# Attention and a gated product on one core: batch 3 as one block of 448 tokens, and a new order on every engine

## The chip, the cores and the metric

The kernel runs on one core of a Trainium2 chip. The metric is the device time of that core in microseconds, taken as the median of several executions. TensorE (PE) does the matrix products, VectorE (DVE), ScalarE (ACT) and GpSimd (POOL) the work on single elements, and SyncE (SP) issues the loads, the stores and the transposes by DMA.

## The reference

Inputs are q, k and v of shape 4 x 12 x 448 x 64 (batch, head, position, width), `w_in` (768 x 2048) and `w_out` (2048 x 768), all float32.

```python
scores = q @ k.T / sqrt(64)            # per batch and head; later positions are masked
attn = softmax(scores)                 # over the keys
x = (attn @ v) laid out as [4*448, 12*64]       # 1792 tokens x 768
h = x @ w_in                           # 1792 x 2048
g = h * (1 / (1 + exp(-1.702 * h)))
out = g @ w_out                        # 1792 x 768
```

## The kernel before

**Precision.** Each large product is done in 16 bits with both factors split into a high and a low part, as three products (high x high, high x low, low x high) that add up in PSUM. The splits are scaled by powers of two taken from sums of squares of the inputs. Weights and inputs are converted and split on DVE and ACT on the way in.

**Tokens and blocks.** The 1792 tokens are 28 chunks of 64, seven in a batch. `TUNE["groups"]` cuts them into nine blocks in this order: 0 = batch 0, chunks 0-3 (256 tokens); 1 = batch 1, chunks 0-2 (192); 2 and 3 = batch 2 (256 and 192); 4 and 5 = batch 3 (256 and 192); 6 = batch 1, chunks 3 and 4 (128); 7 = batch 1, chunks 5 and 6 (128); 8 = batch 0, chunks 4-6 (192). Blocks 0 and 1 do their attention in 32 bits with transposes on PE; the later blocks use 16-bit splits and transposes by DMA.

**Work of a block.** First come six units of attention (`unit`, one per pair of heads): scores on PE (`ps_s`), maxima on DVE (line 1122), exponentials on ACT (line 1136), splitting into `p`, its transpose `PT`, the product with v (`ps_v`, line 1302), and the result as `xT`. Then `moe(n)`: eight times `h_slice`, each for 256 columns of `w_in`, and then `out_tile` for each 128 tokens. One `h_slice` runs two halves `t` of 128 columns, and each half is 18 pairs of matmuls (`halves`, line 410: two matmuls side by side, each on 64 columns of weights) whose width is the number of tokens of the block. Both halves lie in one bank of `ps_h`, so a block of w tokens has 2w columns there, which are then read by four operations: tanh on ACT (line 1401), a multiply on DVE (line 1406), the high part of `gT` on ACT or DVE (468, 470) and its low part on DVE (473). One `out_tile` (line 1442) has two halves `nh` of 384 output columns; each takes 48 pairs of matmuls 384 wide in eight groups of six pairs, and group f needs pair f of the 16 pieces of `w_out`, which `w_out_split` splits on DVE into `wob` (line 473, 128x768).

**Buffers.** `xT` and `gT` are rings of seven chunks; a block sits at `first_at[n] % 7`. `ps_h` has three banks, `ps_o` and `ps_s` two, `PT` two buffers.

**What sets the order.** Each piece of work is an operation with a number. The table `ORDER` lists all of them, each with its engine (S, P, A, D, G for SP, PE, ACT, DVE, POOL); each engine runs its own in that order, and waits at an operation until its inputs are there. All loads go through SP's queue in table order.

Of the kernel before, what the change touches and what calls it, by code (L numbers as in the profile page):

```python
# [49 lines left out]
    wi2=2.63,  # L50
    parts=(((0, 1), (1, 3), (3, 6)), ((0, 3), (3, 6))),
# [3 lines left out]
1D 3G 2A 60S 0G 4S 45S 57S 9S 541G 14S 108S 61P 49S 5A 62A 6D 7A 84P 27S 8D 47S 58P 85A 59A 111S 10D 82P 491S 11A  # L55
46S 70P 12A 83D 13D 15A 159S 63P 71D 162S 73D 16A 109P 64D 447S 66D 74A 17D 93P 444S 72A 110D 65A 18D 86P 67A 75P
77D 96D 19P 28A 78D 94D 32S 87D 133P 89D 97A 20D 29D 79P 48S 95A 76D 21P 68P 88A 112P 22D 90A 30D 80A 98P 24D 100D
23D 113A 31D 134A 432S 121P 69A 101D 25A 99D 135P 122D 114P 124D 50S 91P 136D 123A 160P 115D 117D 125A 144P 26D 118A
436S 116A 137P 161A 163P 92A 102P 145D 164A 215S 147D 184P 146A 140D 210S 128D 148A 186P 138D 494S 129D 185D 141A
119P 103D 434S 172P 33A 187D 165P 139A 34D 81P 538S 173D 35A 168D 126P 166D 433S 175D 188P 169A 151D 120D 195P 167A  # L60
36D 174A 437S 51P 176A 191D 189D 152D 127A 196D 104P 198D 192A 52D 37P 190A 179D 228S 105D 197A 573S 53P 130P 216D
199A 545S 448P 54D 38D 217A 180D 202D 445P 56D 55D 131D 39P 149P 617D 40D 449D 106A 153P 218D 446A 42D 469P 107D
211A 142P 203D 450P 219D 150A 233S 467P 143A 435S 132P 212D 154A 470A 451D 155P 43A 213D 453D 170P 214D 177P 468A
457P 156D 452A 181P 251S 171A 41D 44D 178A 471P 193P 157A 200P 182A 454A 495P 458D 229A 204P 158D 246S 478P 194A
# [12 lines left out]
606A 342S 659D 603A 348S 536A 321D 607P 356A 665P 609D 296D 537D 777S 322D 660A 592P 361A 666P 661D 375S 608A 357D
362A 323P 610D 672P 671D 314D 358D 667A 611P 363D 394A 399S 673P 668D 612A 442D 680D 364D 613P 669A 674P 343A 670D
405S 329P 986D 344A 614D 675P 371D 372D 615A 349D 681P 778S 345A 616D 335P 350D 676A 682P 346D 351A 341P 677D 376A
381S 683P 352D 678A 347P 377D 684P 387S 679D 378A 400D 353P 987P 685A 379D 359P 988P 686D 395A 365P 406D 779S 989P  # L80
687D 396A 1003P 366D 688D 367P 990P 397D 995P 382A 368D 411S 370D 369D 1004P 373D 991A 374D 383D 689A 996P 992D 384D
1005P 993A 690D 780S 388A 997P 385D 1006P 691A 389D 998P 401A 407D 380P 390D 723P 999A 408D 402A 391D 386P 412A 994D
392P 403D 781A 1011P 413A 409D 398P 559S 1012P 1000D 561S 414A 404P 692D 1013P 562S 1001A 415D 410P 1007A 560S 1014P
693A 782D 1002D 417S 724P 784G 1008D 542S 783G 694D 1019P 1009A 786A 543S 1010D 416P 1015A 1020P 428D 721D 788G 787D
695A 725P 1016D 429G 859S 563A 1051D 789G 696D 1021P 856S 1017A 1348D 564P 1027P 697A 857S 1018D 565D 1022P 567D
566G 858S 698D 568A 726P 815S 785G 418D 1023A 1035P 569D 699A 1028P 790S 546A 419D 1036P 547A 700D 420A 727P 1024D
764S 549A 701D 1029P 765S 548A 421D 728P 1025A 570S 860A 702D 422P 1037P 554D 861D 1026D 703A 863G 423D 555P 729P
862D 766S 556D 558D 557G 865A 704D 424P 1043P 763S 775A 867G 425D 866D 1030P 854A 427D 426D 730P 1281D 922S 868G
776D 571A 921S 1044P 430D 855D 802P 924S 705A 791P 1038P 923S 805D 731A 1045P 706D 767A 869S 743P 803D 806A 794D
707A 792D 768P 827P 572D 732S 744P 804A 795A 816P 769D 807G 708D 1046P 793A 1191S 771G 925A 796G 745P 431D 808D  # L90
1031A 1346D 770G 709D 894S 772A 926D 733P 797D 1032D 928G 710D 864G 811A 746P 1193S 798A 927G 800A 773D 809A 734P
711A 1194S 812D 1039A 747P 799D 774S 712D 1033A 735P 1195A 801D 817D 713A 810D 748P 819D 845S 830D 930A 828D 736P
818A 714D 844S 932G 820A 829A 749P 842S 931D 821G 831A 843S 722D 715A 1034D 737P 933G 822D 1040D 1073S 1196A 832G
1052D 750P 716D 823A 1192S 825A 1200A 833D 824D 738P 826D 836A 1076S 1349D 1347D 1361D 751A 834D 837D 717A 881P 813S
835D 1053P 1362D 1041D 1199A 718D 846A 870P 1054P 1075S 882D 1202A 884D 739P 838S 719A 873D 871D 1042D 883A 906P
720D 885A 895P 847P 1055P 1074S 874A 848D 886G 872A 850D 849D 740P 959S 1201A 851D 929G 1198A 875G 887D 1056P 852D
1197A 741A 934S 814P 888A 876D 1203D 890D 1047A 753P 877D 889D 879A 891D 853S 1077A 1057P 907D 909D 908A 878D 754P
880D 910A 896D 1078D 898D 897A 911G 1058P 742S 1048D 899A 1080G 1079D 892S 1049A 1081D 900G 912D 755P 915A 913D
1050D 1082A 1204P 839P 901D 916D 904A 1209S 1084G 756P 914D 902A 1083D 840A 1208S 905D 1059P 1085G 903D 841D 1211S
757P 1205D 917S 1207D 1206G 946P 935P 1929D 758P 1994D 947D 938D 1086S 948A 936D 1060P 949D 939A 2540D 937A 950A  # L100
# [191 lines left out]
def kernel(  # L292
# [1275 lines left out]
```

## Time and profile before

| | |
|---|---|
| time, median of 3 runs | 582.13 us (581.78 to 582.66) |
| the profiled execution's own time | 581.97 us |
| its span | 580.3 us |
| granted TensorE clock | 1.000 |

The span runs from the first to the last instruction of the profiled execution; its own time lies 1.7 us above. An engine's busy time is the time in which at least one of its instructions ran. Matmuls overlap, so what one costs in a stream is read from the starts of successive groups.

### The profile page before, as it was taken

The page shows a single profiled execution, that of the slowest core. Times are in us where ns is not written, and L with a number is a line of the kernel's source. Part 1 is how long each engine was busy: PE and PEld are TensorE (multiplying, and loading weights), DVE is VectorE, ACT ScalarE, POOL GpSimd, SP SyncE. Part 2 cuts the span into 40 slices and gives each one's busy share as a digit, 9 for nine tenths or more (in the row PEclk, how much of TensorE's full clock was granted, in tenths as well). Part 3 has the DMA queues.
Part 4 walks back from the last instruction along what each step waited for, and adds up shares of the span by engine and source line. Part 5 has one row for each costly group of instructions (what it writes and reads, how often), then busy time and mean ns, then how long its engine had stood idle before and what let it go on. Part 6 is the DMA issues. An engine that isn't in the chain of part 4 may idle for free.

```text
span 580.3 us, 24080 instructions
## 1 busy us (share of the span) xinstructions
PE 564.2 (97%) x10376; PEld 475.5 (82%) x10376; DVE 424.6 (73%) x1201; ACT 365.2 (63%) x879; POOL 60.8 (10%) x165
## 2 busy tenths in 40 slices
PE   6999979999999999999999999999999999999997
PEld 4778868988788998779977899778987978889965
DVE  3899999999998688778758759555887987823110
ACT  5899999899976566458746556364665555512210
POOL 2000000013120102101100103011102020000000
PEclk9999999999999999999999999999999999999999
DMA  8999659588997968899846967877758957620010
GB/s 267 268 275 371 199 165 334 180 190 161 187 194 152 155 124 155 141 164 170 155 71 130 154 122 111 130 157 132 119 110 141 139 97 113 107 61 3 16 28 28
DMA packets 228187, 86.70 MB, mean 149 GB/s; under 512 B 208880, under 2 KB 217840, under 8 KB 228080
## 3 DMA queue, kind: packets, MB, share of 16 engines
q1 hardware_dynamic: 228080, 85.16, 72.4%
q8 instruction: 81, 1.33, 1.0%
q14 instruction: 26, 0.21, 0.1%
HBM read 44.63 MB, written 5.51 MB: 86 GB/s over the span
## 4 chain that ended last, share of the span: by engine, by line
PE 78%; DVE 12%; DMA 4%; ACT 2%; issue 1%; SPq 1%; DVEq 0%; ACTq 0%
PE ps_o L1442 33%; PE ps_h L410 30%; PE ps_v L1302 5%; PE ps_s L1099 5%; DVE wob L592 2%; DVE wob L473 2%; PE ps_s L1090 2%; PE ps_o L913 2%; DMA wob<-in_moe_w_out_dram 2%; DMA gT<-in_k_dram 1%; PE ps_h L903 1%; DVE ps_h L1406 1%; DVE wob L558 1%; DMA out_dram<-ob 1%; DVE wob L577 1%
## 5 line engine op out<-in xcount | busy, mean ns | idle before, releaser
L410 PE MATMUL ps_h<-xT,wib 128*64 128x192 f16 (+2 forms) x5184 | 247.7, 249 | 1.2 <-DVE gT L473 0.9
L1442 PE MATMUL ps_o<-wob,gT 128*64 128x384 f16 x2688 | 237.3, 326 | 0.5 <-DVE wob L473 0.5
L410 PEld LDWEIGHTS <-wib 128*64 128x64 f16 x5184 | 224.9, 110 | 10.9 <-issue 3.2
L1442 PEld LDWEIGHTS <-gT 128*64 128x64 f16 x2688 | 153.2, 110 | 54.4 <-issue 0.9
L1136 ACT ACTIVATE z<-z,cols 128x384 f32<-128x384 f32 (+6 forms) x140 | 72.8, 521 | 56.3 <-DVE cols L1122 48.3
L1122 DVE CUSTOM_DVE_ANT_0 z<-ps_s,mask,cols 128x384 f32<-128x384 f32 (+6 forms) x126 | 62.6, 519 | 26.4 <-PE ps_s L1099 25.4
L1401 ACT ACTIVATE t<-ps_h,cols 128x384 f32<-128x384 f32 (+2 forms) x72 | 42.3, 587 | 45.8 <-PE ps_h L410 44.0
L473 DVE SCALAR_TENSOR_TENSOR p<-z,cols,p 128x384 f16<-128x384 f32 (+3 forms) x126 | 67.6, 558 | 3.4 <-ACT p L468 2.7
L1406 DVE SCALAR_TENSOR_TENSOR ps_h<-t,ps_h 128x384 f32<-128x384 f32 (+2 forms) x72 | 41.3, 574 | 37.4 <-ACT t L1401 37.0
L468 ACT ACTIVATE p<-z,cols 128x384 f16<-128x384 f32 (+3 forms) x78 | 41.7, 555 | 9.5 <-DVE cols L1262 4.9
L1099 PE MATMUL ps_s<-kT,qT 128*64 128x384 f16 (+5 forms) x504 | 45.5, 288 | 0.3 <-DMA kT<-kk 0.3
L473 DVE SCALAR_TENSOR_TENSOR gT<-ps_h,gT 128x384 f16<-128x384 f32 (+2 forms) x72 | 40.9, 567 | 6.5 <-ACT gT L468 6.3
L1302 PE MATMUL ps_v<-PT,v 128*64 128x192 f16 (+7 forms) x924 | 42.7, 237 | 0.0
L468 ACT ACTIVATE gT<-ps_h 128x384 f16<-128x384 f32 (+2 forms) x60 | 30.1, 501 | 18.1 <-DVE ps_h L1406 17.2
L468 ACT ACTIVATE ob<-ps_o,cols 128x384 f32<-128x384 f32 x24 | 13.9, 577 | 38.1 <-PE ps_o L1442 35.4
L1302 PEld LDWEIGHTS <-v 128*64 128x64 f16 x828 | 32.8, 110 | 2.1
L1256 POOL TENSOR_SCALAR cols<-cols 128x2 f32<-128x2 f32 (+1 forms) x53 | 14.4, 272 | 158.3 <-ACT z L1136 157.7
L1099 PEld LDWEIGHTS <-qT 128*64 128x64 f16 x504 | 24.5, 110 | 4.7 <-issue 0.4
L1053 POOL TENSOR_SCALAR qq<-qq 128x384 f16<-128x384 f16 (+2 forms) x32 | 20.9, 655 | 54.6 <-ACT qq L468 32.4
L1136 ACT ACTIVATION_READ_ACCUMULATOR z<-z,cols 128x1 f32 x140 | 26.5, 189 | 0.0
L449 POOL TENSOR_SCALAR cols<-cols 128x1 int32<-128x1 int32 x18 | 8.5, 470 | 164.2 <-DVE cols L435 163.9
L470 DVE TENSOR_SCALAR p<-z,cols 128x384 f16<-128x384 f32 (+3 forms) x48 | 22.8, 487 | 1.0
(121 smaller groups left out, 598.5 us busy)
## 6 DMA issues: line engine op xcount, KB each, us to landing
wob<-in_moe_w_in_dram SPq DMA_DIRECT2D x15, 768.0 KB, 7.4
kk<-in_k_dram SPq DMA_DIRECT2D x48, 112.0 KB, 3.3
vraw<-in_v_dram SPq DMA_DIRECT2D x12, 384.0 KB, 5.7
wob<-in_moe_w_out_dram SPq DMA_DIRECT2D x6, 768.0 KB, 6.5
out_dram<-ob SPq DMA_DIRECT2D x22, 192.0 KB, 2.4
p<-in_moe_w_out_dram SPq DMA_DIRECT2D x4, 768.0 KB, 7.1
kk<-in_moe_w_out_dram SPq DMA_DIRECT2D x3, 768.0 KB, 7.9
vraw<-in_moe_w_out_dram SPq DMA_DIRECT2D x3, 768.0 KB, 4.9
```

The source lines that it names most:

```text
L410: nc.tensor.matmul(out[o : o + 64], lhsT[:, o : o + 64], rhs, start=start, stop=stop)
L468: nc.scalar.activation(out=dst, in_=src, func=AF.Copy, scale=sc)
L470: nc.vector.tensor_scalar(out=dst, in0=src, scalar1=sc, scalar2=None, op0=ALU.mult)
L473: nc.vector.scalar_tensor_tensor(out=dst, in0=src, scalar=sc, in1=hi, op0=ALU.mult, op1=ALU.subtract)
L1053: nc.gpsimd.tensor_scalar(out=dst, in0=src, scalar1=1.0, scalar2=1.0, op0=ALU.mult, op1=ALU.mult)
L1099: nc.tensor.matmul(ps[64 * j : 64 * j + 64], qt[:, g, i - c0, 64 * j : 64 * j + 64], kt[:, : i + 1, 64 * j : 64 * j + 64], start=(g == 0), ...
L1122: lambda e: nc.vector.tensor_tensor_reduce(out=z[:, :w], in0=ps, in1=mask[:, S - w :], scale=c, scalar=3.0e38, op0=ALU.add, op1=ALU.min, a ...
L1136: lambda e: nc.scalar.activation(out=z[:, :w], in_=z[:, :w], func=AF.Exp, bias=m, scale=-1.0, accum_out=l),
L1302: nc.tensor.matmul(ps[64 * j : 64 * j + 64, 64 * (first - c0) : w], vt[:, J, j] if f32(gr) else vt[:, gv, J, j, :], (p_f32(pi)[:, at] if f ...
L1401: lambda e: nc.scalar.activation(out=th, in_=ph, func=AF.Tanh, scale=ts[:, sl : sl + 1]),
L1406: lambda e: nc.vector.scalar_tensor_tensor(out=ph, in0=th, scalar=1.0, in1=ph, op0=ALU.add, op1=ALU.mult),
L1442: nc.tensor.matmul(po[64 * j : 64 * j + 64, :OH], gT[:, r, gg, f], wo_pair(f, gw, nh), start=(f == 0 and gg + gw == 0), stop=(f == NFC - 1 ...
```

## The change

`hb` joins blocks for the products with `w_in`: blocks 4 and 5 are one block of 448 tokens there, blocks 6 and 7 one of 256. Attention keeps its nine blocks. For 448 tokens two halves do not fit in a bank of 512 columns, so `h_part` handles one half (448 columns) at a time; for 256 tokens both halves share a bank (512 columns), where before each of blocks 6 and 7 had 256. `moe` of a joined block is called when the attention of its last part is there. The largest scale of `w_in` is worked out once and not twice. The parameters `og`, `ig`, `gram_p`, `ko` and `vg` stand at values under which the code does what it did. `ORDER` is written anew, 2870 operations where there were 2968.

```diff
+    hb=((0,),(1,),(2,),(3,),(4,5),(6,7),(8,)),
...
 ORDER = """
-1D 3G 2A 60S 0G 4S 45S 57S 9S 541G 14S 108S 61P 49S 5A 62A 6D 7A 84P 27S 8D 47S 58P 85A 59A 111S 10D 82P 491S 11A
...
+1D 3G 2A 4S 0G 57S 60S 9S 111S 108S 14S 539G 47S 5A 6A 58P 7A 159S 8D 61P 162S 59A 49S 82P 62A 10A 84P 45S 83A 11D
...
+    parts_of = {ns[0]: ns for ns in TUNE["hb"]}
+    wide = {n: sum(blocks[x][2] - blocks[x][1] for x in ns) for n, ns in parts_of.items()}
...
     def h_slice(n, sl, prio):
 
-        _, c0, c1, gr = blocks[n]
-        w = 64 * (c1 - c0)
+        gr = blocks[n][3]
+        nc_ = wide[n]
+        w = 64 * nc_
         r = first_at[n] % GT
+        nt = 2 if 2 * w <= 512 else 1
+        for t0 in range(0, 2, nt):
+            h_part(n, sl, t0, nt, nc_, w, r, gr, prio + t0 / 2)
+
+    def h_part(n, sl, t0, nt, cn, w, r, gr, prio):
         hb = sl % 2 if n == 0 else ps_h_r.next()
-        ph = ps_h[hb][:, : 2 * w]
+        ph = ps_h[hb][:, : nt * w]
         half = NU // 2
-        for t in range(2):
+        for t in range(nt):
             for a in range(0, NU, half):
 
                 def mm(e, a=a, t=t):
                     for u in range(a, a + half):
                         for gw, gx in ((0, 0), (0, 1), (1, 0)):
                             halves(
-                                ph.rearrange("p (r t x) -> p r t x", t=2, x=64)[:, :, t],
-                                wib[:, sl, u, gw, t * P : (t + 1) * P],
+                                ph.rearrange("p (r t x) -> p r t x", t=nt, x=64)[:, :, t],
+                                wib[:, sl, u, gw, (t0 + t) * P : (t0 + t + 1) * P],
                                 xT[:, gx, u, 64 * r : 64 * r + w],
...
-        if n:
-            moe(n - 1)
-    moe(NB - 1)
+        for x in range(n + 1):
+            if x in parts_of and x not in done and (parts_of[x][-1] < n or wide[x] > 4 or n == NB - 1) and parts_of[x][-1] <= n:
+                done.append(x)
+                moe(x)
```

Three places of the new order follow. Rows give the line, the operation and its tiles; the lines of the changed kernel are 8 to 28 higher than those of before for the same code.

On SP, the first seven loads: of before first (`gT` receives the pieces of q and k in 32 bits, `wob` the raw `w_in`).

```order
L894 DMA gT<-in_q_dram 128x4x128
L650 DMA wob<-in_moe_w_in_dram 128x512
L829 DMA v_69<-in_v_dram 128x4x64
L894 DMA gT<-in_k_dram 128x4x128
L650 DMA wob<-in_moe_w_in_dram 128x2x512
L650 DMA wob<-in_moe_w_in_dram 128x3x512
L894 DMA gT<-in_k_dram 128x4x128
```

And of the change.

```order
L658 DMA wob<-in_moe_w_in_dram 128x512
L910 DMA gT<-in_k_dram 128x4x128
L910 DMA gT<-in_q_dram 128x4x128
L658 DMA wob<-in_moe_w_in_dram 128x2x512
L910 DMA gT<-in_q_dram 128x4x128
L910 DMA gT<-in_k_dram 128x4x128
L658 DMA wob<-in_moe_w_in_dram 128x3x512
```

The first piece of `w_in` has moved ahead of q and k, the second pieces of q and k ahead of the last piece of `w_in`, and v behind all of them.

On DVE, the instructions up to the third-last split of `w_out` (the last row; it is pair 13 of 0 to 15). Before:

```order
L473 SCALAR_TENSOR_TENSOR wob<-wob,cols 128x768
L473 SCALAR_TENSOR_TENSOR qq<-qq,cols 128x8x64
L1362 TENSOR_TENSOR cols<-cols 128x1
L473 SCALAR_TENSOR_TENSOR gT<-ps_h_90,gT 128x3x128
L1262 RECIPROCAL cols<-cols 128x2
L1406 SCALAR_TENSOR_TENSOR ps_h_88<-t_80,ps_h_88 128x384
L1362 TENSOR_TENSOR cols<-cols 128x1
L473 SCALAR_TENSOR_TENSOR wob<-wob,cols 128x768
```

And now:

```order
L478 TENSOR_SCALAR wob<-wob,cols 128x768
L1459 COPY cols<-cols 64x1
L478 TENSOR_SCALAR gT<-ps_h_89 128x3x128
L481 SCALAR_TENSOR_TENSOR wob<-wob,cols 128x768
L1278 RECIPROCAL cols<-cols 128x2
L481 SCALAR_TENSOR_TENSOR qq<-qq,cols 128x8x64
L481 SCALAR_TENSOR_TENSOR p_79<-z,cols,p_79 128x128 x2
L481 SCALAR_TENSOR_TENSOR gT<-ps_h_89,gT 128x3x128
L481 SCALAR_TENSOR_TENSOR wob<-wob,cols 128x768
```

The work of block 1's products (`gT` from `ps_h`) and of attention (`p`) stands ahead of this split in other numbers than before: up to it DVE has 337 instructions (without reads of accumulators) where it had 329.

On PE, the start of batch 3's products with `w_in`. Before, block 4 (256 tokens, written as 4x64) begins behind scores:

```order
L1099 MATMUL ps_s_86<-kT_67,qT_75 64x448
L1099 LDWEIGHTS qT_75
L1099 MATMUL ps_s_86<-kT_67,qT_75 64x448
L410 LDWEIGHTS wib
L410 MATMUL ps_h_88<-xT,wib 64x4x64
L410 LDWEIGHTS wib
L410 MATMUL ps_h_88<-xT,wib 64x4x64
```

Now blocks 4 and 5 begin together, behind an output tile:

```order
L1470 MATMUL ps_o_92<-wob,gT 64x384
L1470 LDWEIGHTS gT
L1470 MATMUL ps_o_92<-wob,gT 64x384
L418 LDWEIGHTS wib
L418 MATMUL ps_h_88<-xT,wib 64x448
L418 LDWEIGHTS wib
L418 MATMUL ps_h_88<-xT,wib 64x448
```

Each weight tile of `w_in` now serves 448 tokens in one matmul, where it was loaded once for 256 and again for 192.

## Rows read from the trace of the kernel before

**Rows 1.** Page, part 1: each engine's busy us, share of the span, instructions.

```profile
PE 564.2 (97%) x10376; PEld 475.5 (82%) x10376; DVE 424.6 (73%) x1201; ACT 365.2 (63%) x879; POOL 60.8 (10%) x165
```

**Rows 2.** Windows: us, busy PE, PEld, DVE, ACT, POOL, PEclk, DMA share, GB/s.

```profile
0.00:12.00 12.00, 6.80 (x50) 4.42 (x51) 2.97 (x11) 5.81 (x11) 3.09 (x19) 1.00 0.81 260
12.00:152.38 140.38, 134.07 (x2530) 112.19 (x2532) 135.58 (x370) 131.89 (x291) 9.97 (x22) 1.00 0.88 237
...
180.00:200.00 20.00, 19.41 (x321) 17.02 (x318) 15.37 (x42) 10.37 (x25) 2.55 (x8) 1.00 0.96 165
...
260.00:280.00 20.00, 20.00 (x448) 18.69 (x444) 17.28 (x67) 16.76 (x56) 2.59 (x8) 1.00 1.07 182
```

**Rows 3.** Timeline, PE: start us, us, line, operation, tiles, count.

```profile
189.67 0.54 PE L1099 MATMUL ps_s<-kT,qT 128*64 128x448 f16 x4
190.05 1.14 PE L1442 MATMUL ps_o<-wob,gT 128*64 128x384 f16 x12
191.03 9.01 PE L410 MATMUL ps_h<-xT,wib 128*64 128x256 f16 x162
199.87 1.00 PE L1302 MATMUL ps_v<-PT,v 128*64 128x192 f16 x24
...
268.16 5.37 PE L410 MATMUL ps_h<-xT,wib 128*64 128x192 f16 x126
273.36 1.14 PE L1442 MATMUL ps_o<-wob,gT 128*64 128x384 f16 x12
...
458.43 4.19 PE L410 MATMUL ps_h<-xT,wib 128*64 128x128 f16 x144
462.45 1.14 PE L1442 MATMUL ps_o<-wob,gT 128*64 128x384 f16 x12
```

**Rows 4.** Timeline, DVE and PE, around the third-last split of w_out.

```profile
151.32 0.55 DVE L473 SCALAR_TENSOR_TENSOR gT<-ps_h,gT 128x384 f16<-128x384 f32 x1
151.79 0.15 DVE L1262 RECIPROCAL cols<-cols 128x2 f32<-128x2 f32 x1
...
152.38 1.01 DVE L473 SCALAR_TENSOR_TENSOR wob<-wob,cols 128x768 f16<-128x768 f32 x1
...
153.38 0.59 DVE L473 SCALAR_TENSOR_TENSOR p<-z,cols,p 128x128 f16<-128x128 f32 x2
...
153.44 1.00 PE L1442 MATMUL ps_o<-wob,gT 128*64 128x384 f16 x10 [0.30 <-DVE wob L473]
```

**Rows 5.** Groups by form: line, engine, operation, count; busy us, mean ns; idle before.

```profile
L410 PEld LDWEIGHTS <-wib 128*64 128x64 f16 x5184 | 224.9, 110 | 10.9 <-issue 3.2
...
L473 DVE SCALAR_TENSOR_TENSOR gT<-ps_h,gT 128x384 f16<-128x384 f32 x32 | 17.7, 553 | 3.4 <-ACT gT L468 3.2
...
L1406 DVE SCALAR_TENSOR_TENSOR ps_h<-t,ps_h 128x512 f32<-128x512 f32 x24 | 16.6, 692 | 6.5 <-ACT t L1401 6.4
...
L558 DVE TENSOR_SCALAR wob<-wob 128x768 uint16<-128x768 uint16 x17 | 10.3, 606 | 0.0
...
L470 DVE TENSOR_SCALAR v<-vraw,cols 128x1024 f16<-128x1024 f32 x7 | 5.3, 752 | 5.6 <-PE ps_v L1302 5.5
...
L470 DVE TENSOR_SCALAR PT<-ps_h 128x512 f32<-128x512 f32 x2 | 1.4, 682 | 0.0
...
L470 DVE TENSOR_SCALAR kT<-ps_o 128x256 f32<-128x256 f32 x3 | 1.3, 425 | 2.0 <-PE ps_o L913 2.0
```

**Rows 6.** Timeline, PE and DVE, at the start of the program.

```profile
3.82 1.12 PE L913 MATMUL ps_o<-ident,gT 128*64 128x128 f32 x8 [3.82 <-DMA gT<-in_q_dram]
...
4.41 0.32 DVE L558 TENSOR_SCALAR wob<-wob 128x256 uint16<-128x256 uint16 x1 [3.49 <-DMA wob<-in_moe_w_in_dram]
...
11.34 0.36 DVE L1122 CUSTOM_DVE_ANT_0 z<-ps_s,mask 128x192 f32<-128x192 f32 x1 [0.65 <-PE ps_s L1090]
```

**Rows 7.** DMA issues: tiles, queue, operation, count, us from issue to landing.

```profile
PT<-p SPq DMA_TRANSPOSE x42, 5.1
```

More of the change, by code (lines that the diff above doesn't have):

```diff
@@ L60 @@
[L60 to L64, printed above, removed]
@@ L423, in all_sum @@
         else:
-            row, key = ps_o[1][:, :1], ("O", 1)
+            row, key = turn[0][:, :1], turn[1]
         half = src.bitcast(BF16)[:, 1:2]
@@ L619, in mm @@
                     )
-        add({"PE": len(blocks) * 0.0585}, mm, [k for _, keys in parts for k in keys], ps_keys, prio)
+        add({"PE": len(blocks) * 0.0398}, mm, [k for _, keys in parts for k in keys], ps_keys, prio)
     def gram_max(ps, ps_key, sq, sq_key, prio, n=64):
@@ L645, in w_in_slice @@
         src = w_in32[:, 2 * s * WS : 2 * (s + 1) * WS].rearrange("(k p) f -> p k f", p=P)
-        for x, y in TUNE["parts"][min(s, 1)]:
+        for x, y in TUNE["parts"][min(s, len(TUNE["parts"]) - 1)]:
             here, there = thirds(a, 2 * x, 2 * y), thirds(t, x, y)
@@ L794, in v_batch @@
         sq, sq_key = col("sqv1", 2)
+        if g in TUNE["vg"]:
+            x = ps_x_r.next()
+            ps = ps_s[x][:, XC:]
+            for j in range(NJ):
+                gram_of([(vraw[:, j : j + 1].rearrange("p j h d -> p j (h d)"), [("vraw", j, 0), ("vraw", j, 1)])], ps, [("X", x)], prio, j == 0, j == NJ - 1)
+            gram_max(ps, ("X", x), sq, sq_key, prio)
+            v_scale(g, sq, sq_key, "X", prio)
+            return
         for j in range(2 * NJ):
@@ L1390, in h_slice @@
                     mm,
-                    [("wi", sl, 0), ("wi", sl, 1)] + [("xT", r + x, u, g) for u in range(a, a + half) for g in range(2) for x in range(c1 - c0)],
+                    [("wi", sl, 0), ("wi", sl, 1)] + [("xT", r + x, u, g) for u in range(a, a + half) for g in range(2) for x in range(cn)],
                     [("H", hb)], 1e6 + prio + t / 2,
@@ L1457, in out_tile, with mm @@
             oi = ob_r.next()
             o = ob[oi]
-            add(
-                {**act(OH, psum=True, ap=1), **dve(OH, ap=1)},
-                lambda e, po=po, o=o, sc=sc: scaled(e, o, po[:, :OH], sc),
-                [("O", pb), sc_key], [("ob", oi)], p0,
-            )
+            cuts = [2 * c for c in TUNE["ko"][nh]]
+            for x, (fa, fz) in enumerate(zip(cuts, cuts[1:])):
+                sc, sc_key = bst[g0]["os", nh, x], bst[g0]["os_key", nh, x]
+                if g1 != g0:
+                    sc, sc_key = col(f"osx{nh}{x}", 2)
+                    for sl, g in ((slice(0, 64), g0), (slice(64, P), g1)):
+                        add(
+                            dve(1),
+                            lambda e, sl=sl, g=g, sc=sc, nh=nh, x=x: nc.vector.tensor_copy(sc[sl], bst[g]["os", nh, x][sl]),
+                            [bst[g]["os_key", nh, x]], [sc_key], p0,
+                        )
+                pb = ps_o_r.next()
+                po = ps_o[pb]
+                for f0 in range(fa, fz, 2):
+                    def mm(e, f0=f0, po=po, nh=nh, fa=fa, fz=fz):
+                        for f in range(f0, f0 + 2):
+                            for gg, gw in ((0, 0), (0, 1), (1, 0)):
+                                for j, r in enumerate(rs):
+                                    nc.tensor.matmul(
+                                        po[64 * j : 64 * j + 64, :OH],
+                                        gT[:, r, gg, f],
+                                        wo_pair(f, gw, nh),
+                                        start=(f == fa and gg + gw == 0),
+                                        stop=(f == fz - 1 and gg == 1),
+                                    )
+                    add(
+                        {"PE": 6 * (OH / 2.4 + 2.5) / 1e3},
+                        mm,
+                        [("wob", nh * NWS + f0 // 2)]
+                        + [("gT", r, f, g) for f in (f0, f0 + 1) for g in range(2) for r in rs],
+                        [("O", pb)] + ([] if pb else [("T", 0), ("T", 1)]), 1e6 + prio,
+                    )
+                if x == 0:
+                    add(
+                        {**act(OH, psum=True, ap=1), **dve(OH, ap=1)},
+                        lambda e, po=po, o=o, sc=sc: scaled(e, o, po[:, :OH], sc),
+                        [("O", pb), sc_key], [("ob", oi)], p0,
+                    )
+                else:
+                    add(
+                        dve(OH, ap=1),
+                        lambda e, po=po, o=o, sc=sc: nc.vector.scalar_tensor_tensor(
+                            out=o, in0=po[:, :OH], scalar=sc, in1=o, op0=ALU.mult, op1=ALU.add
+                        ),
+                        [("O", pb), sc_key], [("ob", oi)], p0,
+                    )
@@ L1475, in moe @@
     def moe(n):
-        _, c0, c1, gr = blocks[n]
+        gr = blocks[n][3]
         for s in range(NWS):
@@ L1486, in moe @@
                 out_scale(gr, nh, n * 100 + 30 - 1e6)
-        for i, tt in enumerate(range(first_at[n] // 2, (first_at[n] + c1 - c0) // 2)):
+        for i, tt in enumerate(range(first_at[n] // 2, (first_at[n] + wide[n]) // 2)):
             out_tile(tt, n * 100 + 40 + i)
@@ L1508, in keys_values @@
             v_pair(gr, u, at(n, u) - TUNE["dv"])
+    done = []
     for n, (b, c0, c1, gr) in enumerate(blocks):
```

413 lines of the change are left out of this document (198 added, 215 removed).

## The prediction

> **What bounds the kernel now.** I read the page's busy times first. PE is busy 564.2 of a span of 580.3 us [rows 1], so at most 16.1 us can come from removing its waits, and anything else must come from less work on PE. The windows tell where the 16.1 us lie [rows 2]. In 0 to 12 us PE is idle for 5.2, in 12 to 152.38 for 6.3, in 180 to 200 for 0.6, and in a later window such as 260 to 280 for nothing; what is left, some 4 us, is the drain at the end and small gaps between 152 and 180. So there are two stages. From about 200 us on PE is full, even in the window in which DVE has 17.28 of 20 us, ACT 16.76, and the DMA engines' share is 1.07. There only PE's work counts. Before 152 us another engine sets the pace: from 12 us to 152.38 DVE is busy 135.58 of 140.38 us and ACT 131.89 [rows 2]. The timeline shows the last place where PE visibly stops for this [rows 4]: at 153.44 a group of output matmuls has waited 0.30 us for the third-last split of `w_out`, which DVE began at 152.38 and ended at 153.39. I call this place the anchor. Up to it DVE's list sets the time; behind it PE's remaining work does. The time is then: when DVE reaches the end of that split, plus the PE work that is still to do, plus the waits behind.
>
> The granted clock is 1.00 in all windows shown, which is the level of 2.4 GHz; no term below comes from the clock.
>
> **The change part by part.**
>
> *Wider products.* I take a pair's cost in a stream from starts [rows 3]. Two pairs 448 wide: (190.05 - 189.67)/2 = 190 ns. 81 pairs 256 wide: (199.87 - 191.03)/81 = 109.1. 63 pairs 192 wide: (273.36 - 268.16)/63 = 82.5. 72 pairs 128 wide: (462.45 - 458.43)/72 = 55.8. A block has 8 slices x 2 halves x 18 = 288 pairs. Blocks 4 and 5 cost 288 x (109.1 + 82.5) = 55.2 us and now 288 x 190 = 54.7. Blocks 6 and 7 cost 2 x 288 x 55.8 = 32.1 and now 288 x 109.1 = 31.4. That is -1.2 us, in the stage where PE is full, so all of it counts. The 448 figure comes from two pairs only and from other operands; 2 ns more or less would be 0.6 us. The rows show why it is so little: a pair's time is nearly in proportion to its width, and half the matmuls are not half the time.
>
> The weight loads behind these matmuls take 110 ns each [rows 5], longer than the 55.8 ns of a 128-wide pair, yet the pairs follow each other at 55.8, so loads are hidden here. The Trainium skill, "TensorE: Matmul & The Clock Gate", section "Back-to-back issue gap", says the opposite for a stream of loads and matmuls: about 81 ns each at 128 columns and 131 at 512, while N/2.4 + 2.5 is only the isolated gap; by its figures (an estimate) blocks 6 and 7 would go from 576 x 81 = 46.7 us to 288 x about 98 = 28.2. Our rows follow the isolated formula at every width (128/2.4 + 2.5 = 55.8), so the trace disagrees with the page and the sum goes by the rows.
>
> *Reading the wider banks.* Blocks 4 and 5 had 8 banks of 512 and 8 of 384 columns; now 16 of 448. Blocks 6 and 7 had 16 of 256, now 8 of 512. One part of 448 takes PE 18 x 190 = 3.4 us; its four readers take at most 0.69 us each even at 512 columns on DVE [rows 5], some 2.8 in a row, and there are three banks. PE's next two parts, 6.8 us, hide it: cost nothing. If that cover were gone, each of 16 parts would cost up to 2.8 us.
>
> *DVE's list up to the anchor.* Counting the two orders up to the third-last split, DVE gains six high or low parts of `gT` at 384 columns (6 x 0.553), three conversions of 768 (3 x 0.606), one more split of 768 (1.01), one scaling of v (0.752) and two `p` (0.59 together): 7.5 us. It loses one multiply at 512 columns (0.692), two `PT` copies (2 x 0.682), two copies of 256 (2 x 0.425) and one conversion of 256 (0.32): 3.2 us [rows 4 to 6]. Instructions overlap by 0.08 us (the one at 151.32 ends at 151.87, the next starts at 151.79 [rows 4]), and there are 8 more, so the net is 4.3 - 0.6 = +3.6 us.
>
> *PE's list up to the anchor.* Ahead of the same group of matmuls PE now has three more groups of an output tile, each six pairs of 384: 3 x 0.98 = 2.9 us ((191.03 - 190.05) for one group [rows 3]). Work that is done before the anchor is not left behind it. Together: +3.6 - 2.9 - 1.2 = **-0.5 us**.
>
> *DVE's idle time before the anchor.* It is 9.0 us in 0 to 12 and 4.8 in 12 to 152.38 [rows 2]. At the start two things go against each other. PE's first transposes wait until 3.82 for q, the first load; the second load lands at 4.41 [rows 6]. Now `w_in` is first and k second, so they start at about 4.4, and DVE's first maxima, at 11.34 before, come up to 0.6 us later. In return the next q and k no longer stand behind the large third piece of `w_in`, so the next units find their inputs. After 12 us DVE's partner in most chains is ACT, and ACT's list up to the anchor adds up to the same as before while DVE's is 3.6 us longer; so ACT is ahead more often and DVE should wait for it less. No row prices this. Bounds: three of the 4.8 us saved (-3), or the late start and as much again of new gaps (+2). I take **-0.5**, near the middle, since the 4.8 us are 3% and leave little to win.
>
> *Waits behind the anchor.* 0.6 us in 180 to 200 [rows 2]; with the output groups in another order, half of it may go: **-0.3** (bounds -0.6 and +0.6).
>
> *The rest.* The largest scale of `w_in` is worked out once: two instructions of the 0.15 us kind [rows 4], on engines that have slack there. The queues SP and POOL carry the same loads; SP has the same 335 operations.
>
> Sum: -0.5 - 0.5 - 0.3 = -1.3 us on the profiled execution's 581.97, which lies 0.16 under the median of 582.13: **580.7 us**. What a measurement here can tell from no change is about 0.2%, 1.2 us: below 580.8 is faster, above 583.1 slower.
>
> **The rivals.**
>
> *No change.* The anchor's -0.5 stands, but the late first maxima and the new gaps on DVE cost 1 to 2 us: 581.0 to 583.1, and at the outer bounds (+2 and +0.6) 584.1. For it: DVE has 3.6 us more before the anchor, and the start is later by the rows. Against it: DVE has only 4.8 us of gaps to begin with and ACT's pressure does not grow.
>
> *Slower: attention behind the joined block runs dry.* The joined block holds all seven chunks of `xT` until its last slice, so the results of blocks 6 to 8, 18 units, are written only after it. PE has some 100 us of work between the end of that slice and the last product with v (output tiles of batch 3, the products of blocks 6 and 7, attention): 5.5 us for a unit. A transpose of `p` takes 5.1 us to land [rows 7], and maxima, exponentials and splitting stand ahead of it, all with two buffers. If a unit's chain cannot be spread over two units' time, 11 us, PE stops each time; at 0.5 us a unit that is 9 us: 580.7 + 9 = about 590. It decides from the point where PE's list offers less than the missing time as ready work between two units. For it: units stand closer than before. Against: in 260 to 280, where DMA is at 1.07 and DVE at 17.28, PE lost nothing, and output tiles of 96 x 163 ns = 15.6 us stand between [rows 3].
>
> *Weight loads pace the narrow products.* If 110 ns per pair [rows 5] were their true price, blocks 6 and 7 would drop from 576 x 110 = 63.4 us to 31.7, and the time to about 549. Rows 3 speak against it: they show the pairs at 55.8. The page named above would be the rule behind this.
>
> **How the numbers follow.** Forecast 0.55, its own range 578.0 to 581.5; no change 0.26; dry attention 0.16, with 584 to 592; weight loads 0.03. The range 577.5 to 584.0 holds the forecast and the no-change case with their bounds (581.97 - 0.5 - 3 - 0.6 = 577.9; 581.97 - 0.5 + 2 + 0.6 = 584.1), some 0.8. Faster by over 0.2%: four fifths of the forecast case, the last rival and a little of the second, 0.50. Within 0.2%: the rest of the forecast and two thirds of the second, 0.28. Slower: dry attention and the upper end of the second, 0.22.
>
> **What would show it.** Right: pairs 448 wide follow at about 190 ns and 256 at 109; PE's busy time falls by about 1.2 plus what waits change; the third-last split starts near 155.5 (152.38 + 3.6 - 0.5), and the PE group behind it has waited under 1 us; no PE waits from 200 us on. Wrong: first maxima after 12 us with DVE idle more than 6 us from 12 us to the anchor (no change); PE waiting for `PT`, `xT` or `ps_v` between 390 and 500 us (dry attention); pairs of 448 well above 190, or a wait for `ps_h` in the joined block (the readers are not hidden).

## The result: 0.8% slower, and the profile after

The changed kernel takes 587.25 us (586.48 to 588.77, 6 runs) where the kernel before, run beside it, takes 582.39: ratio 1.0081, 95% interval 1.0054 to 1.0107. The forecast of 580.7 and its range up to 584.0 are missed, on the slow side.

The page of the changed kernel, part 1, which answers to [rows 1]. PE is busy for 1.2 us more, in a span that is 5.2 us longer, with 1152 matmuls fewer:

```profile
PE 565.4 (97%) x9224; PEld 496.4 (85%) x9224; DVE 413.3 (71%) x1157; ACT 366.6 (63%) x876; POOL 62.5 (11%) x178
```

The windows by stretch say where the time is. The columns are those of [rows 2]; an engine's idle time is a window's length less its busy time. First the kernel before, up to the start of its third-last split:

```profile
0.00:20.00 20.00, 14.80 (x152) 9.97 (x154) 10.23 (x39) 12.73 (x33) 3.09 (x19) 1.00 0.95 257
20.00:60.00 40.00, 39.59 (x720) 31.13 (x716) 37.78 (x137) 37.43 (x107) 0.00 (x0) 1.00 1.03 317
60.00:100.00 40.00, 35.97 (x680) 31.01 (x678) 39.16 (x91) 39.85 (x72) 0.00 (x0) 1.00 0.72 222
100.00:152.38 52.38, 50.51 (x1042) 44.49 (x1038) 51.39 (x114) 47.69 (x92) 9.97 (x22) 1.00 0.84 184
```

Then the changed kernel up to the same split, and two windows of its full stage:

```profile
0.00:20.00 20.00, 14.05 (x132) 9.88 (x132) 8.26 (x39) 11.10 (x33) 3.10 (x19) 1.00 1.00 266
20.00:60.00 40.00, 39.67 (x702) 30.88 (x702) 35.98 (x127) 35.29 (x101) 0.00 (x0) 1.00 0.99 280
60.00:100.00 40.00, 36.51 (x656) 30.89 (x652) 39.61 (x91) 38.10 (x72) 0.00 (x0) 0.96 0.66 211
100.00:161.14 61.14, 56.57 (x1148) 50.91 (x1145) 59.00 (x132) 54.34 (x107) 11.99 (x24) 1.00 0.93 200
...
200.00:300.00 100.00, 100.00 (x1828) 94.52 (x1824) 78.61 (x242) 72.45 (x190) 16.80 (x43) 1.00 0.96 159
300.00:400.00 100.00, 100.00 (x1305) 81.60 (x1303) 74.81 (x210) 62.01 (x151) 15.45 (x50) 1.00 0.74 132
```

From 200 us on PE is full again, the joined block (300 to 400) included. The loss lies ahead of the third-last split of `w_out`. DVE's busy time up to it goes from 138.56 to 142.85 us, +4.3, which is the longer list; its idle time goes from 13.8 to 18.3, +4.5: +2.0 in the first 20 us, +1.8 from 20 to 60, -0.5 from 60 to 100, +1.2 behind. Together the split starts 8.8 us later. The timeline of the changed kernel, DVE and PE, which answers to [rows 4]:

```profile
161.14 1.00 DVE L481 SCALAR_TENSOR_TENSOR wob<-wob,cols 128x768 f16<-128x768 f32 x1
...
162.20 1.00 PE L1470 MATMUL ps_o<-wob,gT 128*64 128x384 f16 x10 [1.15 <-DVE wob L481]
```

PE now waits 1.15 us at the anchor where it waited 0.30. From the anchor to the last copy of the output it takes 582.12 - 162.20 = 419.9 us; before, 576.89 - 153.44 = 423.5. So 3.5 of the 8.8 us come back, near the -4.1 that the forecast had for the work done ahead and the wider products. The last copy on ACT in the changed kernel:

```profile
582.12 0.58 ACT L476 ACTIVATE ob<-ps_o,cols 128x384 f32<-128x384 f32 x1 [0.39 <-PE ps_o L1470]
```

### The profile page after: what moved, and what is told of

It is laid out like the page before. It is cut to its first block, busy times and chain, and to the rows that moved or that the text cites. A ratio compares the mean times of both kernels' runs of the same rounds, so it can differ in the third digit from the quotient of the medians.

```text
span 585.5 us, 21770 instructions
## 1 busy us (share of the span) xinstructions
PE 565.4 (97%) x9224; PEld 496.4 (85%) x9224; DVE 413.3 (71%) x1157; ACT 366.6 (63%) x876; POOL 62.5 (11%) x178
## 4 chain that ended last, share of the span: by engine, by line
PE 82%; DVE 10%; DMA 3%; ACT 2%; issue 1%; SPq 1%; POOL 0%; DVEq 0%; ACTq 0%
PE ps_o L1470 33%; PE ps_h L418 31%; PE ps_v L1318 5%; PE ps_s L1115 5%; PE ps_o L929 2%; PE ps_s L1106 2%; DVE wob L600 2%; PE ps_h L919 1%; DMA wob<-in_moe_w_out_dram 1%; DVE wob L481 1%; DMA kk<-in_k_dram 1%; DVE wob L566 1%; DVE wib L481 1%; DVE wob L585 1%; DVE v L481 1%
## 5 line engine op out<-in xcount | busy, mean ns | idle before, releaser
L418 PE MATMUL ps_h<-xT,wib 128*64 128x256 f16 (+2 forms) x4032 | 243.6, 273 | 0.4 <-DVE gT L481 0.2
L418 PEld LDWEIGHTS <-wib 128*64 128x64 f16 x4032 | 209.7, 110 | 18.5 <-issue 2.8
L1470 PEld LDWEIGHTS <-gT 128*64 128x64 f16 x2688 | 182.8, 110 | 30.4 <-issue 4.0
L1429 DVE SCALAR_TENSOR_TENSOR ps_h<-t,ps_h 128x512 f32<-128x512 f32 (+2 forms) x64 | 40.0, 625 | 66.6 <-ACT t L1424 66.3
L1138 DVE CUSTOM_DVE_ANT_0 z<-ps_s,mask,cols 128x384 f32<-128x384 f32 (+6 forms) x126 | 62.2, 517 | 17.8 <-PE ps_s L1115 16.1
L1424 ACT ACTIVATE t<-ps_h,cols 128x512 f32<-128x512 f32 (+2 forms) x64 | 40.3, 629 | 40.4 <-PE ps_h L418 38.3
L476 ACT ACTIVATE p<-z,cols 128x512 f16<-128x512 f32 (+3 forms) x83 | 44.5, 561 | 17.2 <-DVE cols L1278 10.1
L481 DVE SCALAR_TENSOR_TENSOR gT<-ps_h,gT 128x512 f16<-128x512 f32 (+2 forms) x64 | 39.7, 620 | 12.4 <-ACT gT L476 11.9
L476 ACT ACTIVATE gT<-ps_h 128x512 f16<-128x512 f32 (+2 forms) x54 | 29.4, 545 | 18.8 <-DVE ps_h L1429 18.6
L600 DVE SCALAR_TENSOR_TENSOR wob<-wob 128x768 int32<-128x768 int32 (+2 forms) x23 | 21.0, 915 | 4.5 <-ACT wob L581 4.5
L457 POOL TENSOR_SCALAR cols<-cols 128x1 int32<-128x1 int32 x18 | 4.4, 242 | 179.9 <-DVE cols L443 179.2
```

The source lines that it names most:

```text
L418: nc.tensor.matmul(out[o : o + 64], lhsT[:, o : o + 64], rhs, start=start, stop=stop)
L476: nc.scalar.activation(out=dst, in_=src, func=AF.Copy, scale=sc)
L481: nc.vector.scalar_tensor_tensor(out=dst, in0=src, scalar=sc, in1=hi, op0=ALU.mult, op1=ALU.subtract)
L600: lambda e: nc.vector.scalar_tensor_tensor(out=words(dst, I32, 1)[..., 0], in0=words(raw, I32, 2)[..., 1], scalar=3, in1=words(dst, I32, 1 ...
L1138: lambda e: nc.vector.tensor_tensor_reduce(out=z[:, :w], in0=ps, in1=mask[:, S - w :], scale=c, scalar=3.0e38, op0=ALU.add, op1=ALU.min, a ...
L1424: lambda e: nc.scalar.activation(out=th, in_=ph, func=AF.Tanh, scale=ts[:, sl : sl + 1]),
```

## Experiments

Most of them cross the two orders: one kernel's code, one order up to a cut, the other behind it. In the diffs the first line of the table shows whose order leads, the later one is the line with the cut, given with how many entries stand ahead of it. The numbers of operations differ a little between the two codes (539G and 541G are the same operation). The change was 1.0081 of the kernel before; an experiment is given as the ratio to the runs of the kernel before on its own chip, with its 95% interval. "Split" is the start of the third-last split of `w_out` on DVE in the profile: 152.38 before, 161.14 after.

### Which half of the change costs the time

`e1_old_ramp`: the changed code, 948 entries in the order of before.

```diff
-1D 3G 2A 4S 0G 57S 60S 9S 111S 108S 14S 539G 47S 5A 6A 58P 7A 159S 8D 61P
+1D 3G 2A 60S 0G 4S 45S 57S 9S 539G 14S 108S 61P 49S 5A 62A 6D 7A 84P 27S
...
+836S 717A 871D 869D 1040D 881A 904P 718D 1045A 1046D 1047D 1195A 1196A 750S 1048D 1072S 1053P 1054P 883A 845P
```

> The changed kernel with its joined blocks, but up to the last split of w_out (about 160 us) every engine runs the operations in the order of the kernel before, and then what is left in the changed order. Theory (DVE stands idle some 5 us longer in the new order of the first 60 us, and the join itself is worth -1.3 us): about 581, between 580 and 582.5, third-last split near 152.4. Rival (the joined block costs the time behind 300 us): 586 or more, third-last split near 152.4 but waits of PE between 300 and 500.

Measured: 582.61 us, ratio 0.9992 (0.9970 to 1.0014), split 151.99. The loss is gone, joined blocks and all. The expected gain is not seen either, though the interval does not exclude it: between 152 and 200 PE is now idle for 3.8 us where it was 1.05 before. Windows of this kernel and then its PE waits behind 145 us (us in total, times, longest):

```profile
152.00:200.00 48.00, 44.20 (x666) 38.82 (x663) 38.41 (x138) 32.83 (x99) 4.95 (x17) 1.00 0.96 168
```

```profile
PE ps_v L1320 <- DMA PT<-p: 1.8, 1, 1.8
PE ps_o L1472 <- ACT ob L478: 1.0, 2, 0.7
```

These 2.8 us stand behind the cut, between 160 and 181 us.

`e2_new_ramp`: the code of before, 959 entries in the changed order.

```diff
-1D 3G 2A 60S 0G 4S 45S 57S 9S 541G 14S 108S 61P 49S 5A 62A 6D 7A 84P 27S
+1D 3G 2A 4S 0G 57S 60S 9S 111S 108S 14S 541G 47S 5A 6A 58P 7A 159S 8D 61P
...
+717A 1075S 835D 846A 1076S 881P 718D 870P 1056P 838S 1202A 884D 719A 882D 739P 873D 871D 885A 720D 883A
```

> The kernel before with nine separate blocks, but up to the last split of w_out in the order of the changed kernel, then in its own. Theory (first part of the order): about 588, between 586.5 and 589.5, since it has the late splits and not the join's -1.3; third-last split near 161. Rival (joined block): 582 to 583.

Measured: 587.81 us, ratio 1.0078 (1.0047 to 1.0108), split 160.48. With no joined block at all the kernel loses as much as the whole change. The rival of the joined block falls in both directions.

### Where in the first 160 us

`e3_old_20`, `e4_old_60` and `e7_old_105` are the changed code with the order of before for 21, 62 and 105 us; `e8_new_105` is the code of before with the changed order for 105 us. The first lines of the tables are those shown above; the lines with the cut are, in this sequence, behind 105, 397, 620 and 623 entries:

```diff
+91P 136D 123A 160P 115D 492S 144P 125A 163P 117D 161A 147D 116A 145D 164A 148A 118A 137P 146A 172P
...
+574P 300S 485P 270A 634P 630D 484A 271A 259D 575D 500P 261D 642D 486D 635P 631A 542S 333A 636P 637P
...
+1001P 686D 1002P 368D 369P 993P 396A 370D 372D 371D 988P 373D 374D 397D 687A 1003P 719D 994P 1049D 382A
...
+989P 406A 395D 779S 396A 367P 990P 397D 995P 382A 368D 411S 370D 369D 373D 991A 374D 383D 689A 996P
```

> The changed kernel with only the operations of the first 21 us in the order of before (the first loads on SP among them). Theory: the 2.0 us of idle DVE time that the first 21 us add come back, so about 585.2, between 584 and 586; third-last split near 159. Rival (DVE's longer list ahead of the splits is the cause, not its gaps): 587, split at 161. Rival (joined block): 587.

Measured: 588.95 us, ratio 1.0095 (1.0066 to 1.0124), split 162.84: a miss. DVE's idle time in the first 20 us falls from 11.7 to 9.5 us, but it is 15.5 by 40 us where the changed kernel has 14.3: new gaps stand behind the cut. The run decides neither for the theory nor for its rivals.

> The changed kernel with the operations of the first 62 us in the order of before. Theory: some 4.1 us of idle DVE time come back, so about 583, between 582 and 584.5; third-last split near 157, since the 3.6 us of additional DVE work ahead of it stay. Rival (the longer list is the cause): 587. Rival (joined block): 587.

Measured: 586.06 us, ratio 1.0058 (1.0037 to 1.0079), split 159.23. DVE is idle for 11.6 us up to 60 (15.8 in the changed kernel) and for 14.9 up to 80 (16.1): of 4.1 us saved, 2.9 are lost behind the cut. What comes back is a third (by time) to a half (by the split) of what was expected.

> The changed kernel in the order of before for the first 105 us, a place where both orders have done almost the same operations (they differ by five). Theory (3.3 us of the gaps arise before 105 us): third-last split near 158.3, time about 584.3, between 583 and 585.5. Rival (what costs time is the order between 105 and 160, with its longer list): split near 161, 587.

Measured: 585.54 us, ratio 1.0047 (1.0030 to 1.0064), split 158.20, as expected for the split; the time is just above the range.

> The kernel before with the changed order for the first 105 us only. Theory: the same 3.3 us of gaps, third-last split near 155.2, time about 585.3, between 584.3 and 586.3. Rival (order between 105 and 160): split near 152, 582.5.

Measured: 587.50 us, ratio 1.0082 (1.0058 to 1.0105), split 157.26. The new order of the first 105 us alone costs the kernel before 4.9 us at the split and 5.4 in time, more than the 3.3 expected; its DVE gaps are 3.4 us longer up to 100 us and 4.5 up to 160.

So both stretches carry a share, and cuts add to it: the two shares (5.8 and 4.9 us at the split) add up to more than the whole. The windows up to the split, first of `e7_old_105` and then of `e8_new_105`, tell the two causes apart:

```profile
0.00:158.20 158.20, 144.30 (x2620) 121.22 (x2621) 143.07 (x388) 139.74 (x309) 15.10 (x43) 1.00 0.89 235
0.00:157.26 157.26, 143.31 (x2578) 119.78 (x2580) 138.87 (x377) 136.79 (x303) 13.90 (x41) 0.98 0.87 230
```

With the old order first, DVE is busy for 143.07 us and idle for 15.1; with the changed order first, 138.87 and 18.4; before, 138.56 and 13.8. So the longer list comes with the order behind 105 us, and most of the idle time with the order of the first 105 us; the 1.3 us more of idle time in `e7_old_105` are within what kernels of one order differ by (last section). What holds in all of these runs is the rule of the forecast. Span less split is 427.9 before and 430.1 and 428.1 in `e1_old_ramp` and `e8_new_105`, where PE has the old work ahead of the split; it is 424.4 after, and 424.6, 424.0, 424.7 and 424.2 in `e2_new_ramp`, `e3_old_20`, `e4_old_60` and `e7_old_105`, where three more groups lie ahead of it.

### The start

`e6_loads` moves one load of the changed kernel; `e11_start` moves the four conversions that need it too.

```diff
-1D 3G 2A 4S 0G 57S 60S 9S 111S 108S 14S 539G 47S 5A 6A 58P 7A 159S 8D 61P
+1D 3G 2A 0G 57S 60S 4S 9S 111S 108S 14S 539G 47S 5A 6A 58P 7A 159S 8D 61P
...
+1D 3G 2A 0G 57S 60S 4S 9S 111S 108S 14S 539G 47S 58P 159S 61P 162S 59A 49S 82P
```

> The changed kernel with one load moved on SP: the first piece of w_in goes behind the first pieces of k and q. Theory (the late first k costs DVE 1.0 to 1.2 us that stays lost): PE starts near 3.8 and not 4.99, first maxima near 11 and not 12.03, third-last split 1 us earlier, time 586.2. Rival (a gap saved at the start is only made again later, because DVE waits for other engines in the next 40 us anyway): first maxima near 11, but split and time within 0.5 us of the changed kernel, 587.

Measured: 587.62 us, ratio 1.0093 (1.0077 to 1.0110), split 162.71. Neither theory: PE does start at 4.14, but then stands for 2.02 us, because ACT's queue has the conversion of the load that now comes third ahead of the copy of `kT`. PE's timeline of this kernel:

```profile
4.14 1.97 PE L931 MATMUL ps_o<-ident,gT 128*64 128x128 f32 x16 [4.14 <-POOL vraw L791]
8.13 1.12 PE L931 MATMUL ps_o<-ident,gT 128*64 128x128 f32 x8 [2.02 <-ACT kT L478]
```

A load and the first instruction that waits for it on an in-order engine have to move together.

> The changed kernel with the first piece of w_in behind the first pieces of k and q on SP, and its three conversions on ACT and one on DVE behind the first copies of kT and qT, so that ACT's queue no longer holds these copies up. Theory (a gap saved at the start stays saved): first maxima near 11.0 and not 12.03, third-last split near 160.1, time 586.2. Rival (the gap is only moved to the next tens of us): first maxima near 11.0, split within 0.4 us of 161.1, time 587.2.

Measured: 586.49 us, ratio 1.0057 (1.0037 to 1.0077), split 158.18. The first maxima are at 11.14 and DVE's idle time in 20 us is 10.6 and not 11.7. By ratios this gives back 0.24% of the 0.81%, with intervals that overlap. For the start, the theory of gaps that stay saved is favoured, not settled: the profiled execution (584.10) is the fastest of its six, and its split is 1.9 us earlier than expected.

### The join by itself

`e9_join_185` and `e10_join_172` are the changed code with the order of before for 185 and 172 us (1132 and 1066 entries); `e5_late_join` for some 300 us (1872 entries), up to the first product of batch 3. Lines with the cut:

```diff
+1212D 1064P 1214D 1213G 1088A 1215D 1091G 1296P 1216D 1060S 1097P 1134A 1092D 1093A 1095D 1094D 1096D 1394S 1098D 956P
...
+942D 958P 750S 950D 969P 943D 1059A 891P 941D 951A 959D 953D 960A 961D 952D 1210A 954D 1131S 970D 962A
...
+1816D 2101S 1706P 1810D 1817A 2102S 1818D 1714P 1707A 1811S 1819A 1826P 2090A 1881S 1820G 1827D 2091P 1828A 2092D 1821D
```

> The joined blocks, with the order of before for the first 185 us, the place where the two orders differ least in what has been done by then. Theory (the join is worth 1.2 us, the first part of the order costs the rest, and the run with the cut at 160 lost its gain to waits at the cut): third-last split near 152.4, 0.3 us or less of new waits, time 1.2 us under before, ratio 0.998. Rival (the changed order behind 185 has waits of its own): ratio 1.000 or more with waits of PE behind 200.

Measured: 583.35 us, ratio 1.0012 (0.9999 to 1.0025), split 153.20. Not the gain expected: PE waits 1.8 us for `cols` and 0.6 more around the cut, between 182 and 191 us.

> The same with the cut at about 172 us, the second-best place. Theory: ratio 0.998 to 0.999, third-last split near 152.4. Rival: 1.000 or more.

Measured: 589.33 us, ratio 1.0115 (1.0090 to 1.0141), split 155.06. One wait of 6.4 us of PE for a sum of squares from DVE (`cols`) stands behind the cut. A place where the orders have done nearly the same is not yet a good seam.

> The changed kernel in the order of before up to the first product of batch 3 with w_in (about 300 us), then in the changed order: the join with nothing else in the first half. Theory (join worth 1.2 to 1.5 us of PE work, no waits behind 200): 581.2 where before is near 582.6, ratio 0.9975, and PE never waits after 200. Rival (the change of order inside the full stage, or the joined block, brings waits): 583 or more, with waits of PE behind 300.

Measured: 601.11 us, ratio 1.0313 (1.0290 to 1.0335). It is the most telling miss. PE's windows and its waits from 318 to 352 us, in the order of before up to the joined block:

```profile
320.00:340.00 20.00, 12.47 (x162) 9.87 (x159) 15.38 (x40) 12.27 (x29) 2.05 (x8) 0.82 0.96 164
340.00:360.00 20.00, 15.46 (x193) 11.83 (x194) 15.44 (x41) 9.35 (x24) 4.09 (x9) 0.84 0.94 153
```

```profile
329.77 1.38 PE L1117 MATMUL ps_s<-kT,qT 128*64 128x384 f16 x8 [1.88 <-DMA qT<-qq]
...
337.24 1.60 PE L1117 MATMUL ps_s<-kT,qT 128*64 128x384 f16 x8 [3.42 <-DVE cols L1140]
...
341.86 1.81 PE L1320 MATMUL ps_v<-PT,v 128*64 128x192 f16 x24 [1.62 <-DMA PT<-p]
```

Before, the 31 us of products of block 4 (288 x 109.1 ns) ran on PE while DVE, ACT and the DMA queues did the attention of block 5. A joined block cannot start until block 5's attention is done, so this work no longer covers it: PE is idle for 12 us here, and the granted clock is 0.82 and 0.84 in the mean of these windows, so for a part of them at its lower level (0.50, 1.2 GHz) and not at the upper one (1.00, 2.4 GHz). How much of the 12 us is the seam's own, as in `e10_join_172`, no run separates. The changed order avoids this in the full stage, where it has no wait, with attention that stands earlier.

`e12_no_join` is the code of before in the whole changed order, with separate products in the places of the joined ones. A line around the first product of block 4:

```diff
+2115S 1837A 2048D 2064P 2071P 2113S 1715P 1924D 1838D 2116S 1708P 2065D 1925S 2072D 2066A 1716P 2049D 2073A 2067G 1930P
```

> The kernel before (nine separate blocks) with the whole order of the changed kernel; where a joined block's products stand there, the separate blocks' products stand one after the other. This prices the join alone. Theory (join worth -1.2 us by pairs, and it brings no waits): 588.4, ratio 1.0105 to before, third-last split near 161. Rival (the join brings waits that eat its gain): 587 or less. Where PE waits for a bank of ps_h in blocks 6 and 7, which the joined blocks' order does not serve well, that is taken off.

Measured: 603.55 us, ratio 1.0354 (1.0334 to 1.0374), split 162.15. Between 300 and 400 us, in blocks 4 and 5, PE has no wait. Behind 400 the places of the joined blocks 6 and 7 serve 128-token products badly: PE waits 8.4 us for `ps_h` and 2.4 for `cols`. Taking some 11 us off leaves 592, which is above the changed kernel, but the correction is larger than the effect. So the time of this run does not price the join; its trace does for batch 3, as the next section reads it.

## Why the prediction was wrong

**The step that failed** is "DVE's idle time before the anchor", taken as -0.5 with bounds of -3 and +2. It measured +4.5 in the two profiles (from 9.0 to 9.9 us up to 12 us, and from 4.8 to 8.3 behind), and +3.3 between the means of the kernels that share either order (last section). The reason given for the minus sign, that ACT would be ahead more often and DVE would wait for it less, did not come true. DVE's waits of the changed kernel in the first 60 us (us in total, times, longest), the four largest that name ACT, without the one of 4.5 us for the first pieces of `w_in`; then, before, the only one that names ACT, which is of the kind left out:

```profile
DVE qT L478 <- ACT kT L476: 4.3, 2, 2.6
...
DVE ps_v L1341 <- ACT qq L1152: 1.1, 1, 1.1
DVE ps_v L1341 <- ACT PT L476: 0.6, 1, 0.6
DVE qT L478 <- ACT qq L1152: 0.5, 1, 0.5
```

```profile
DVE wob L592 <- ACT wob L573: 1.0, 1, 1.0
```

The first row's 4.3 us are two copies out of PE's late transposes. Each starts 0.03 us after a copy by ACT ended, which had itself waited for PE (0.67 and 1.47 us), so they belong to the start. The other three rows, 2.2 us, are for ACT's exponentials and copies. From 100 us to the split, too, DVE's waits for ACT grew, from 0.2 to 1.5 us. ACT's total work ahead of the anchor being the same said nothing about where its instructions stand. The idle time was priced as a total of 4.8 us that could only shrink or grow by a part; in fact a new order makes its own gaps.

**The start** was seen but priced too low. Its bound of 0.6 us was for the first maxima: PE started at 4.99, not 4.4, and the maxima came at 12.03 (+0.7). The second unit lost more, behind 16 transposes instead of 8: its maxima begin at 15.67 us and not at 14.78. Timelines of the changed kernel, PE and DVE:

```profile
4.99 1.98 PE L929 MATMUL ps_o<-ident,gT 128*64 128x128 f32 x16 [4.99 <-DMA gT<-in_k_dram]
12.43 1.97 PE L929 MATMUL ps_o<-ident,gT 128*64 128x128 f32 x16
```

```profile
12.03 0.36 DVE L1138 CUSTOM_DVE_ANT_0 z<-ps_s,mask 128x192 f32<-128x192 f32 x1
...
14.87 0.43 DVE L478 TENSOR_SCALAR qT<-ps_o 128x256 f32<-128x256 f32 x1 [1.78 <-ACT kT L476]
```

**The anchor** was right as the place and as the rule: the end is the split plus the PE work behind it, in the changed kernel and, where PE does not wait long behind it, in the crossed orders. DVE's longer list was right in kind, +3.6 forecast and +4.3 of busy time measured, which is the forecast's own figure before it took 0.6 off for overlaps. PE's 2.9 us of work done ahead was near: `e2_new_ramp`, without a joined block, has a span less split of 424.6, which is 3.3 us under before.

**The wider products** were right by the price of a pair. PE's timeline of the changed kernel: 9 pairs of 448 columns take 337.20 - 335.50 = 1.70 us, 189 ns each (190 forecast).

```profile
335.50 1.90 PE L418 MATMUL ps_h<-xT,wib 128*64 128x448 f16 x18
337.20 0.68 PE L1115 MATMUL ps_s<-kT,qT 128*64 128x256 f16 x8
```

Eleven hundred matmuls fewer are thus worth about 1.4 us by pairs. Two readings show it as PE's time. The changed kernel and `e12_no_join` run the same PE work from the first product of batch 3 to the attention behind its last one, with PE full but for the one wait shown; first the end of this stretch in the changed kernel, then start, a wait and end in `e12_no_join`:

```profile
401.77 0.62 PE L1318 MATMUL ps_v<-PT,v 128*64 128x128 f16 x18
```

```profile
335.89 2.16 PE L412 MATMUL ps_h<-xT,wib 128*64 128x256 f16 x36
...
401.56 0.62 PE L1304 MATMUL ps_v<-PT,v 128*64 128x128 f16 x18 [0.42 <-DVE xT L475]
...
403.47 0.62 PE L1304 MATMUL ps_v<-PT,v 128*64 128x128 f16 x18
```

It takes 401.77 - 335.50 = 66.27 us with the joined block and 403.47 - 335.89 - 0.42 = 67.16 without: the block of 448 saves 0.9 us. For all joins, PE's busy time behind the split can be compared: 423.3 and 423.4 us before and in `e8_new_105`, 422.6 and 422.8 with joined blocks in `e1_old_ramp` and `e9_join_185`; and with three more groups ahead of the split 419.8 in `e2_new_ramp` and 418.4 to 418.9 in the changed kernel, `e3_old_20`, `e4_old_60`, `e6_loads`, `e7_old_105` and `e11_start`. So the joins save some 0.6 us of PE's time by the first comparison and 1.2 by the second, where the forecast had 1.2. As a faster kernel no run shows it: in `e1_old_ramp` and `e9_join_185` waits behind the cut are larger than it. The forecast's sign that PE's busy time would fall by 1.2 us did not come: it rose by 1.2, since it is 4.7 us less behind the split but 5.9 more ahead of it, where PE is not full; 2.9 of these are the three groups, the rest is not explained. The weight-load rival is out, at 189 ns for a pair of 448 and with no large gain. **The waits behind the anchor** were forecast at -0.3; from the anchor to 200 us PE is idle for 1.3 us, where it was 0.75, so they grew by 0.5.

**The rivals.** The slower one that was named, dry attention behind the joined block, did not happen in the changed kernel: PE has no wait from 200 us on. A like mechanism shows on the near side of the join: `e5_late_join` shows a joined block whose preceding attention has no cover, in a kernel 19 us slower, with 12 us of idle PE time there. The outcome was the no-change rival's mechanism, late first maxima and new gaps on DVE, beyond its bounds; both signs named for it came, first maxima after 12 us and more than 6 us of idle DVE time from 12 us to the anchor (8.3).

## What to carry to other kernels

When a change rewrites the order of a stage in which two engines are nearly full, the idle time of that stage is an unknown of its own, and the rows of before don't bound it: as a rule of thumb that no run here tests, give it bounds as wide as the stage's present idle time (13.8 us here), with no preferred sign. Joining two blocks to save instructions on a saturated engine can cost the cover that one block's products gave the other's preparation; ask first what will run in that time. A pair's price per column tells at once that fewer and wider matmuls save little: 1152 fewer gave 1.4 us by pairs and 0.6 to 1.2 us of PE's busy time.

## What was not expected of the hardware

The same instructions in the same order do not start alike. Five profiled kernels share the order of before up to the split; it starts at 151.99, 152.38, 153.20, 154.79 and 155.06 us (`e1_old_ramp`, before, `e9_join_185`, `e5_late_join`, `e10_join_172`), and DVE's idle time in their first 20 us is 10.1, 9.8, 10.2, 10.6 and 11.7. `e9_join_185` and `e10_join_172` ran on one chip, so it is not only the chip. Three with the new order have 160.48, 161.14 and 162.15. So the 8.8 us between the two profiles shown are 7.8 between means: 4.5 of DVE's busy time and 3.3 of its idle time up to the split (14.9 and 18.2; the five with the order of before differ by up to 2.7). Single profiles are not to be compared to a microsecond here.

In the changed kernel the granted clock is at the lower level (0.50, 1.2 GHz) for some 3 us near 82 to 86, behind two waits of PE of 1.03 and 1.55 us:

```profile
80.15 0.19 PE L422 MATMUL ps_o<-cols 128*64 128x1 bf16 x2 [1.03 <-DVE cols L634]
81.89 0.56 PE L1217 MATMUL ps_h<-ident,cols 64*64 64x64 f32 x12 [1.55 <-DVE cols L1291]
```

```profile
82.00:84.00 2.00, 2.00 (x30) 1.71 (x31) 2.00 (x4) 2.00 (x4) 0.00 (x0) 0.65 0.04 14
84.00:86.00 2.00, 2.00 (x36) 1.50 (x34) 2.00 (x5) 2.00 (x4) 0.00 (x0) 0.50 0.04 8
```

DVE and ACT are full there, so PE is not what sets the pace, and the loss does not come from this: `e1_old_ramp`, whose clock is 0.54 and 0.61 in the windows from 84 to 88 us, has the earliest split of all. Nor do the times of the kernel before go with the clock: one of its runs has a mean clock of 0.997 at 580.71 us and another 1.000 at 584.76.
